# Attention with a gated feed-forward gate on one Trainium2 core: four-head groups outermost, transposes by DMA, 64-row scores and queries, and an opening by row tiles

## The chip, the cores and the metric

The kernel runs on one core of one Trainium2 chip. The time is the device time of a run in microseconds. In the profile PE is TensorE (matmuls), PEld its weight loads, DVE VectorE, ACT ScalarE, POOL GpSimd, SP the engine that only issues DMA. Runs of one kernel agree within 0.4%.

A profile shows one run; its span is the time from the first to the last instruction. The measured time of a run is a little longer than its span (957.23 against 955.5 us in the profiled run of the changed kernel).

## The reference, cut to what matters

```python
xn = layernorm(x)                                  # x: 2048 x 640, no affine part
q  = xn @ wq                                       # 32 heads of 192
k, v = k_cache[:, :, -512:], v_cache[:, :, -512:]  # the last 512 of 2048 positions
s  = softmax(q k^T / sqrt(192)) v  per head, then @ wo        # 6144 x 640
h  = sigmoid(xn @ w_gate) * (xn @ w_up)            # 640 x 1536 each
g  = silu(h @ w_down)
return x + s * g                                   # bf16 in and out
```

## The kernel before

It works in four blocks of 512 rows. A first part computes the layer norm, turns it (features onto the partitions) on TensorE, and does the whole gated feed-forward part. Then, block by block and inside a block head pair by head pair, `stage1` loads the pair's keys, values and query weights, makes the queries and turns the keys on TensorE; `stage_qk` makes scores and exps; `stage_pv` the weighted values. After the 16 pairs of a block `phase_a2` turns the outputs on TensorE and projects them. A head has 192 features: 128 of them are contracted in one full matmul, the remaining 64 in a matmul on 64 rows, and the two heads of a pair put their 64 rows into different halves of the array.

```python
    def stage1(st, hp, pair_idx):
        ...                                       # DMA: keys and values of two heads, 384 columns of wq
        for j in range(3):
            for c in range(NCD):                  # NCD = 5
                nc.tensor.matmul(q_ps[:], lhsT=wqp[:, c, j * P:(j + 1) * P],
                                 rhs=xnT_sb[:, c * 512:(c + 1) * 512], ...)
        ...
        for c in range(KC):                       # KC = 4: 12 key transposes a pair, in every block
            cb = c * 2 * DH
            for i in range(2):
                nc.tensor.transpose(kA_ps[:, i, c * P:(c + 1) * P], kt[:, cb + colA[i]:cb + colA[i] + P], ident[:])
            nc.tensor.transpose(kB_ps[:, c * P:(c + 1) * P], kt[:, cb + KPAD + P:cb + KPAD + 2 * P], ident[:])

    def stage_qk(st, ctxd):
        for c0 in range(0, KC, 2):
            for c in (c0, c0 + 1):
                for i in range(2):                # 4 matmuls of 128 rows
                    nc.tensor.matmul(S_ps[(c, i)][:], lhsT=kA[:, c * P:(c + 1) * P], rhs=qA_[:], start=True, stop=False)
            for c in (c0, c0 + 1):
                for i in range(2):                # 4 matmuls of 64 rows, heads in different halves
                    nc.tensor.matmul(S_ps[(c, i)][:], lhsT=kB[:, c * P:(c + 1) * P], rhs=qB_, start=False, stop=True)
            ...                                   # 4 exps of 512 columns

    def phase_a2(st):
        for q in range(TQ):
            for fq in range(NG):                  # 12 groups of 4
                for j in range(4):
                    nc.tensor.transpose(pT[:, j, :], o_st[q][:, cc * P:(cc + 1) * P], ident[:])
                ...                               # copy pT to oT, by VectorE and ScalarE in turn
                for j in range(4):
                    for (d0, dsz), oA_ps in zip(d_chunks, oA):    # 512 and 128 columns
                        nc.tensor.matmul(oA_ps[:], lhsT=oT[:, j, :], rhs=wo_sb[:, cc, d0:d0 + dsz], ...)
```

The softmax here doesn't subtract the row's maximum and nothing guards it: scores larger than these inputs give would overflow.

## Time and profile before

The median of three runs is 1075.28 us (1073.35 to 1076.93).

| | value | view |
|---|---|---|
| span | 1071.9 us | page |
| TensorE busy, ScalarE, VectorE | 97%, 48%, 41% | page, part 1 |
| chain of waits on TensorE | 82% | page, part 4 |
| until the first gate matmul | 11.76 us | timeline |
| one head pair | 9.64 us | timeline, distance of equal places |

The groups of instructions of the page, in the columns line, engine, operation, output and inputs, shape and count, then busy time and mean ns of one, then the idle time in front of them:

```profile
PE 1034.7 (97%) x7927; PEld 608.0 (57%) x8048; DVE 439.9 (41%) x1163; ACT 515.0 (48%) x981; POOL 113.9 (11%) x163
...
L236 PE MATMUL q_ps<-xnT_a,wqp 128*128 128x512 bf16 x901 | 214.9, 379 | 5.4 <-DMA wqp<-in_A_wq_dram 2.2
...
L343 PE MATMUL pTo<-ident,o_st 128*128 128x128 bf16 x768 | 54.0, 219 | 0.0
...
L254 PE MATMUL kA_ps<-ident,k_sb 128*128 128x128 bf16 x512 | 49.7, 219 | 0.0
L258 PE MATMUL kB_ps<-ident,k_sb 128*128 128x128 bf16 x256 | 46.2, 219 | 0.0
```

The lengths of matmuls overlap in the profile (their ends are modelled): a matmul of 379 ns is followed by the next after some 216 ns. What a matmul costs in a stream is the distance from start to start. The timeline of one score stage (start and length in us, then the instructions) shows it:

```profile
416.18 0.38 PE L286 MATMUL S_ps<-qT_3939,kTA 128*128 128x512 bf16 x1
...
416.39 0.38 PE L286 MATMUL S_ps<-qT_3955,kTA 128*128 128x512 bf16 x1
...
416.82 0.38 PE L286 MATMUL S_ps<-qT_3955,kTA 128*128 128x512 bf16 x1
...
417.13 0.60 PE L293 MATMUL S_ps<-qT_3947,kTB 64*128 64x512 bf16 x4
...
417.67 0.39 PE L286 MATMUL S_ps<-qT_3939,kTA 128*128 128x512 bf16 x1
```

Full 512-column matmuls start 0.21 us apart (0.2158 in the unbroken runs of query matmuls). The fourth full one starts at 416.82, but the first 64-row one only at 417.13, 0.31 us later. The four 64-row matmuls, two at a time, should take two such distances, 0.43 us; the next full one starts after 0.54. Each change between 128-row and 64-row matmuls so costs about 0.1 us in which nothing streams. The Trainium skill has this in "TensorEngine Tiling (Array Packing)", Key Properties: changing the tiling mode drains TensorE. It gives no figure; this trace does.

### The profile page before, as it was taken

The page shows a single profiled execution, that of the slowest core. Times are in us where ns is not written, and L with a number is a line of the kernel's source. Part 1 is how long each engine was busy: PE and PEld are TensorE (multiplying, and loading weights), DVE is VectorE, ACT ScalarE, POOL GpSimd, SP SyncE. Part 2 cuts the span into 40 slices and gives each one's busy share as a digit, 9 for nine tenths or more (in the row PEclk, how much of TensorE's full clock was granted, in tenths as well). Part 3 has the DMA queues.
Part 4 walks back from the last instruction along what each step waited for, and adds up shares of the span by engine and source line. Part 5 has one row for each costly group of instructions (what it writes and reads, how often), then busy time and mean ns, then how long its engine had stood idle before and what let it go on. Part 6 is the DMA issues. An engine that isn't in the chain of part 4 may idle for free.

```text
span 1071.9 us, 19547 instructions
## 1 busy us (share of the span) xinstructions
PE 1034.7 (97%) x7927; PEld 608.0 (57%) x8048; DVE 439.9 (41%) x1163; ACT 515.0 (48%) x981; POOL 113.9 (11%) x163
## 2 busy tenths in 40 slices
PE   6899999999999999999999999999999999999997
PEld 3445445556556665656556555656566555656664
DVE  4654333444454123544452224544432244544322
ACT  2654223666656114666653235666641165666321
POOL 4211002400010001000010010000000010000000
PEclk9999999999999999999999999999999999999999
DMA  9621002975555013555552024555521054451010
GB/s 303 196 93 50 13 37 77 343 205 130 135 127 163 20 38 78 133 144 131 137 144 65 20 71 127 129 144 132 136 70 38 20 147 127 129 144 50 1 38 13
DMA packets 153578, 115.18 MB, mean 107 GB/s; under 512 B 138000, under 2 KB 140560, under 8 KB 153488
## 3 DMA queue, kind: packets, MB, share of 16 engines
q1 hardware_dynamic: 138048, 53.63, 20.3%
q0 software_dynamic: 15440, 60.30, 18.8%
q8 instruction: 63, 1.03, 0.4%
q14 instruction: 27, 0.22, 0.1%
HBM read 106.04 MB, written 7.86 MB: 106 GB/s over the span
## 4 chain that ended last, share of the span: by engine, by line
PE 82%; issue 10%; DMA 3%; ACT 2%; POOL 2%; DVE 1%; POOLq 0%; DVEq 0%
PE q_ps L236 18%; PE o_ps L315 17%; PE S_ps L286 11%; PE S_ps L293 6%; PE kA_ps L254 3%; ACT oT L348 2%; PE pTo L343 2%; DMA xnT_d<-xnT_sb 1%; PE kB_ps L258 1%; PE g_ps L160 1%; PE u_ps L167 1%; PE oA_ps_4443 L352 1%; PE oA_ps_10299 L352 1%; PE oA_ps_13091 L352 1%; PE oA_ps_7371 L352 1%
## 5 line engine op out<-in xcount | busy, mean ns | idle before, releaser
L236 PE MATMUL q_ps<-xnT_a,wqp 128*128 128x512 bf16 x901 | 214.9, 379 | 5.4 <-DMA wqp<-in_A_wq_dram 2.2
L352 PEld LDWEIGHTS <-oT 128*128 128x128 bf16 x1536 | 115.3, 98 | 102.4 <-DVE oT L346 11.8
L328 DVE TENSOR_SCALAR o_st<-o_ps,rden 128x192 bf16<-128x192 f32 x384 | 148.3, 415 | 9.0
L348 ACT ACTIVATE oT<-pTo 128x512 bf16<-128x512 bf16 x96 | 53.8, 595 | 203.2 <-PE pTo L343 203.2
L236 PEld LDWEIGHTS <-wqp 128*128 128x128 bf16 x960 | 92.4, 97 | 100.8 <-DMA wqp<-in_A_wq_dram 2.7
L321 DVE RECIPROCAL rden<-o_ps 128x2 f32<-128x2 f32 x256 | 41.6, 162 | 192.9 <-PE o_ps L315 192.9
L346 DVE COPY oT<-pTo 128x512 bf16<-128x512 bf16 x96 | 40.7, 424 | 178.5 <-PE pTo L343 177.9
L228 POOL DMA_DIRECT2D wqp<-in_A_wq_dram x64 | 55.9, 874 | 472.5 <-PE q_ps L236 428.2
L326 ACT ACTIVATE o_st<-o_ps,rden 128x192 bf16<-128x192 f32 x128 | 54.0, 422 | 66.1 <-DVE o_st L328 61.2
L286 PEld LDWEIGHTS <-kTA 128*128 128x128 bf16 x512 | 42.1, 97 | 57.4 <-issue 26.7
L265 ACT ACTIVATE kTB<-kB_ps 128x512 bf16<-128x512 bf16 x64 | 38.2, 597 | 70.1 <-PE kB_ps L258 70.1
L160 PE MATMUL g_ps<-xnT_sb,wg_sb 128*128 128x512 bf16 x236 | 62.3, 384 | 1.8 <-DVE xnT_sb L154 1.3
L167 PE MATMUL u_ps<-xnT_sb,wu_sb 128*128 128x512 bf16 x233 | 60.8, 382 | 0.2
L173 ACT ACTIVATE sig_sb<-g_ps 128x512 bf16<-128x512 f32 x48 | 28.1, 597 | 60.9 <-PE g_ps L160 60.4
L174 DVE TENSOR_TENSOR hT_sb<-u_ps,sig_sb 128x512 bf16<-128x512 f32 x48 | 32.9, 690 | 53.8 <-PE u_ps L167 44.4
L343 PE MATMUL pTo<-ident,o_st 128*128 128x128 bf16 x768 | 54.0, 219 | 0.0
L254 PEld LDWEIGHTS <-k_sb 128*128 128x128 bf16 x512 | 42.0, 98 | 15.1
L343 PEld LDWEIGHTS <-o_st 128*128 128x128 bf16 x768 | 45.8, 98 | 7.6
L254 PE MATMUL kA_ps<-ident,k_sb 128*128 128x128 bf16 x512 | 49.7, 219 | 0.0
L258 PE MATMUL kB_ps<-ident,k_sb 128*128 128x128 bf16 x256 | 46.2, 219 | 0.0
L293 PEld LDWEIGHTS <-kTB 64*128 64x128 bf16 x512 | 14.6, 94 | 54.2 <-issue 54.2
L180 PEld LDWEIGHTS <-hT_sb 128*128 128x128 bf16 x384 | 29.8, 98 | 26.7 <-DVE hT_sb L174 3.5
(1006 smaller groups left out, 1839.0 us busy)
## 6 DMA issues: line engine op xcount, KB each, us to landing
wqp<-in_A_wq_dram POOLq DMA_DIRECT2D x64, 480.0 KB, 4.6
k_sb<-in_A_k_cache_dram SPq DMA_DIRECT2D x128, 192.0 KB, 4.8
wo_sb<-in_A_wo_dram POOLq DMA_DIRECT2D x16, 480.0 KB, 9.7
v_sb_96<-in_A_v_cache_dram SPq DMA_DIRECT2D x22, 192.0 KB, 2.9
v_sb_98<-in_A_v_cache_dram SPq DMA_DIRECT2D x22, 192.0 KB, 2.9
v_sb_100<-in_A_v_cache_dram SPq DMA_DIRECT2D x21, 192.0 KB, 2.9
v_sb_102<-in_A_v_cache_dram SPq DMA_DIRECT2D x21, 192.0 KB, 2.9
v_sb_104<-in_A_v_cache_dram SPq DMA_DIRECT2D x21, 192.0 KB, 2.9
```

The lines of the kernel that those rows point to most:

```text
L160: nc.tensor.matmul(g_ps[:], lhsT=wg_sb[:, c, f * P:(f + 1) * P], rhs=xnT_sb[:, c * 512:(c + 1) * 512], start=(c == 0), stop=(c == NCD - 1),)
L167: nc.tensor.matmul(u_ps[:], lhsT=wu_sb[:, c, f * P:(f + 1) * P], rhs=xnT_sb[:, c * 512:(c + 1) * 512], start=(c == 0), stop=(c == NCD - 1),)
L236: nc.tensor.matmul(q_ps[:], lhsT=wqp[:, c, j * P:(j + 1) * P], rhs=xnT_sb[:, c * 512:(c + 1) * 512], start=(c == 0), stop=(c == NCD - 1),)
L254: nc.tensor.transpose(kA_ps[:, i, c * P:(c + 1) * P], kt[:, cb + colA[i]:cb + colA[i] + P], ident[:],)
L258: nc.tensor.transpose(kB_ps[:, c * P:(c + 1) * P], kt[:, cb + KPAD + P:cb + KPAD + 2 * P], ident[:],)
L286: nc.tensor.matmul(S_ps[(c, i)][:], lhsT=kA[:, c * P:(c + 1) * P], rhs=qA_[:], start=True, stop=False,)
L293: nc.tensor.matmul(S_ps[(c, i)][:], lhsT=kB[:, c * P:(c + 1) * P], rhs=qB_, start=False, stop=True,)
L315: nc.tensor.matmul(o_ps[:, ii, 0:DH + 1], lhsT=E[i][:, c, q * P:(q + 1) * P], rhs=vt[:, c, 0:DH + 1], start=(c == 0), stop=(c == KC - 1),)
L328: nc.vector.tensor_scalar_mul(dst, o_ps[:, ii, 0:DH], rden[:, ii:ii + 1])
L343: nc.tensor.transpose(pT[:, j, :], o_st[q][:, cc * P:(cc + 1) * P], ident[:])
L348: nc.scalar.activation(oT[:], pT[:], AF.Copy)
L352: nc.tensor.matmul(oA_ps[:], lhsT=oT[:, j, :], rhs=wo_sb[:, cc, d0:d0 + dsz], start=(cc == 0), stop=(cc == NC_O - 1),)
```

## The change

The intent: take every transpose but the first block's off TensorE; load and turn each head's keys once instead of once per block, by putting groups of four heads outermost and the row blocks inside; contract all 192 features of a score in three steps of 64, two heads side by side, and split the query contraction likewise, so that TensorE changes its tiling twice per unit (four heads, 512 rows) instead of eight times for the same work; write the issue order by hand, with the projection of the unit before between the values of this one; begin with 128-row tiles, so that the first matmuls need one tile of x and one slice of weights. The diff, cut to its core:

```diff
+    ctx.enter_context(tc.manual_schedule())
+    bank = [psum.tile([P, 2, 512], F32, name=f"bank{i}") for i in range(4)]
+    def load_group(g):
+        d["wq"] = load2.tile([P, NCD, GW], BF16, name="wq_sb")
+        nc.gpsimd.dma_start(d["wq"][:], wq_r[:, :, g * GW:(g + 1) * GW])
+        ...                                  # one DMA for the keys of four heads, four for the values (GpSimd's queue)
+        for h in range(4):
+            nc.gpsimd.tensor_copy(kp[:, h // 2, :, :, (h % 2) * H2:(h % 2) * H2 + H2], ...)   # feature order 3 x 64
+    def turn_keys(g):
+        for pr in range(2):
+            for c in range(KC):
+                nc.sync.dma_start_transpose(d["kT"][:, pr, :, c * P:(c + 1) * P], d["kp"][:, pr, c, :, :]...)
 ...
-            nc.gpsimd.dma_start(wg_sb[:, :, f0:f1], wg_r[:, :, f0:f1])
-            nc.gpsimd.dma_start(wu_sb[:, :, f0:f1], wu_r[:, :, f0:f1])
+        for q in range(NF // 2):
+            load_slice(nc.scalar, wu_sb, wu_r, q)          # all six slices of w_up from ScalarE
+            if q:
+                load_slice(nc.sync, wg_sb, wg_r, q)
 ...
+        dummy(22)                                          # matmuls on zeros
+        ...
+        for t in range(TQ):                                # block 0: 128-row tiles, 4 of 12 feature groups
+            for f in range(FT): ...
+        for f in range(FT, NF):                            # block 0: the other 8, 512 rows
+            gated(0, f, 0, TB, k, norm_piece(1, f - FT))   # with half a tile's layer norm of block 1
+        load_group(0)
+        for b in range(1, NB): ...
 ...
+    def scores(u, pr, c, k):
+        for j in range(DJ):                                # DJ = 3
+            for i in range(2):
+                r = slice(i * H2, (i + 1) * H2)
+                nc.tensor.matmul(bank[k][:, i, :], lhsT=kT[r, pr, j, c * P:(c + 1) * P],
+                                 rhs=q[r, pr * DJ + j, :], start=(j == 0), stop=(j == DJ - 1))
+        nc.scalar.activation(E[u, pr][:, c, :, :], bank[k][:], AF.Exp, scale=scale_qk)   # 1024 columns
+    def queries(u, m, k, second):
+        for c in range(NCD):
+            for i in range(2):
+                half = i ^ second
+                n = 2 * m + half
+                col = (n // DJ) * 2 * DH + n % DJ
+                r = slice(i * H2, (i + 1) * H2)
+                nc.tensor.matmul(bank[k][:, half, :], lhsT=wq[r, c, col:col + DJ * (P - 1) + 1:DJ],
+                                 rhs=xnT[r, b, c, :], start=(c == 0 and not second), ...)
+    def turn_out(u):
+        for q in range(TQ):
+            nc.sync.dma_start_transpose(oT[u][:, :, q * P:(q + 1) * P], o_st[u][:, q, :])
 ...
+    for u in range(NU):                                    # 32 units
+        for i, what in enumerate(((0, 0), (1, 0), (0, 1), (1, 1), (2, 0), None, (2, 1), None)):
+            scores(u, *sc[i], i % 2)
+            if what is not None:
+                queries(u + 1, what[0], 2 + what[0] % 2, what[1])
+        ...
+            for q in range(4):
+                values(u, q, order[2 * q])
+                if u > 0:
+                    project(u - 1, q, order[2 * q + 1], nc.sync)
+            turn_out(u)
+    ...                                                    # last unit: project(u - 1, 1..3) after the values
```

## The prediction

> **What bounds it now.** TensorE. The page gives PE 97% busy of 1071.9 us, DVE 41%, ACT 48%; the cores view a clock of 0.999; the chain of waits is 82% PE. The timeline gives the pace: 512-column matmuls start 0.2155 us apart, 512+128 pairs of the output projection 0.272, 193-column value matmuls 0.085, transposes 0.056. Times the counts: queries 960 x 0.2155 = 207 us; scores 166 (512 full ones, and 512 on 64 rows that run two at once); values 173; output projection 209; gate and up 103; down 52; transposes 1596 x 0.056 = 89. Sum 999 us. The other 73 us are gaps: the opening until the first gate matmul (11.8 us in the timeline), a few waits (2.7 us at 44 us, a query-weight load that blocks from 182.9 to 190.5 us), about 0.1 us at each change between 128-row and 64-row matmuls (in the timeline 0.31 instead of 0.216 us going in, 0.54 instead of 0.43 for the four 64-row ones going out), and the end. The Trainium skill (TensorEngine Tiling (Array Packing), Key Properties) says a change of tiling mode drains TensorE; this trace agrees: four changes per head pair cost 0.41 us, over 64 pairs 26 us.
>
> **What changes.**
> - Removed from TensorE: 768 key transposes, 768 output transposes and 60 of 80 layer-norm transposes go to DMA: 1576 x 0.056 = 88 us.
> - Mode changes fall from 256 to about 64, because all scores and queries of a unit use 64 rows: 26 to about 6.5 us. 1536 + 1860 half matmuls, two at once, equal the full ones they replace.
> - Keys, values and query weights are loaded once, not four times; off the path but for that one stall.
> - Exps become 1024 wide, estimated at 0.6 + 512 x 0.83 ns = 1.03 us; eight per unit, 8.3 us against 11.7 us of score and query matmuls. DVE has about 11 us of work in a 23.5 us unit. Neither should bind before the last unit.
> - Added: waits for DMA transposes. They have half a unit (about 12 us) of slack, but block 1's last one is issued about 1 us before it is needed: estimate 2 to 3 us lost.
>
> **Sum.** 999 - 88 = 911 us of stream; opening about 9 plus 4 for weights that arrive late; block 1's wait 2.5; mode changes 6.5; small waits in 32 units 5; end 8 (exp-bound last scores, the last transpose, last output DMA). 946 us span; the measured time lies 3 us over the span. I predict 948 us, range 925 to 985. Nearly all removed time is critical, as PE is the chain.
>
> Chances: faster by over 2% 0.97, within 2% 0.02, slower 0.01.
>
> **What would show it.** PE's instruction count without the 1536 transposes; a unit of about 24 us repeated in the timeline; 64-row matmuls two per 0.216 us through a whole score-and-query phase; no PE idle blamed on ACT or DVE above a few us in the waits; DMA transposes landing in under 8 us; DMA traffic well below 115 MB.
>
> **What would make it wrong.** The query weights are now read with a column step of 3 and two 64-row loads per 0.216 us; no load in this trace is strided, and if they can't hide behind the matmuls, queries (a fifth of the time) slow down: +20 to +60 us. Long runs of 64-row pairs may not hold the pace that four show here. DMA transposes, all in one queue, four per unit, may take longer than the 12 us of slack. The opening may wait longer for weights.

## The result, and the profile after

The changed kernel takes 955.23 us (median of four runs, 954.33 to 957.23), the one before 1074.85 us in the same rounds. The ratio is 0.8885, with a 95% interval from 0.8869 to 0.8901. Ratios here are the mean time of one kernel's runs over that of the other's in the same rounds, so not quite the ratio of the medians quoted beside them. 948 us were predicted, and the range of 925 to 985 us holds the result.

The page after, in the same columns as before:

```profile
PE 924.1 (97%) x7965; PEld 551.0 (58%) x8045; DVE 470.6 (49%) x754; ACT 304.2 (32%) x339; POOL 131.6 (14%) x161
...
L360 PE MATMUL bank<-xnT,wq_sb 64*128 64x512 bf16 x1860 | 231.4, 376 | 0.0
...
L342 PE MATMUL bank<-qT,kT 64*128 64x512 bf16 x1536 | 202.4, 376 | 2.0 <-DVE o_st L383 1.3
L377 PE MATMUL bank<-vbuf,E 128*128 128x193 bf16 x2048 | 191.1, 247 | 0.0
```

The transpose groups are gone from TensorE. A matmul on 64 rows is recorded with the same 376 ns as a full one with 379; what tells is how close they lie, in the timeline of one score and query phase:

```profile
504.00 1.24 PE L360 MATMUL bank<-xnT,wq_sb 64*128 64x512 bf16 x10
505.08 1.46 PE L342 MATMUL bank<-qT,kT 64*128 64x512 bf16 x12
506.38 1.24 PE L360 MATMUL bank<-xnT,wq_sb 64*128 64x512 bf16 x10
507.46 0.81 PE L342 MATMUL bank<-qT,kT 64*128 64x512 bf16 x6
508.20 1.51 PE L377 MATMUL bank<-vbuf,E 128*128 128x193 bf16 x16
...
518.43 1.79 PE L400 MATMUL bank<-wo_sb,oT 128*128 128x512 bf16 x12
520.16 0.82 PE L342 MATMUL bank<-qT,kT 64*128 64x512 bf16 x6
```

Ten 64-row query matmuls, with their ten strided weight loads, take 1.08 us from start to start (505.08 minus 504.00): five times 0.216, so two at once for the whole phase. Twelve score matmuls take 1.30 us, six times 0.216. Only at the two ends is there a gap: the last six score matmuls should end at 507.46 + 0.65 = 508.11, the values start at 508.20; the projection that starts at 518.43 lasts 1.63, the scores start at 520.16. A unit repeats every 23.72 us (400.00 minus 376.28 in the chain of waits, for equal places); the matmuls of a unit alone are 54 x 0.2158 + 4 x 1.335 + 4 x 1.63 = 23.5 us (24 pairs of score matmuls and 30 of query matmuls, four heads' values, four projections). There is nothing left to win in a unit but the 0.2 us of the two changes of tiling.

What the prediction had not seen stands at the beginning. The waits, one line for each pair of instruction and what released it (total us, times, longest):

```profile
ACT xnT L207 <- DMA wu_sb<-in_B_w_up_dram: 8.9, 1, 8.9
PEld L221 <- DMA xnT<-xn: 11.6, 1, 11.6
PE bank L221 <- DMA xnT<-xn: 11.1, 1, 11.1
PE bank L221 <- DVE xnT L208: 5.7, 3, 4.9
```

TensorE waits once for a transpose of the layer norm, 11.1 us (its own line has 11.1, that of its weight load 11.6). And ScalarE waits 8.9 us, before the copy of the first turned tile, for a load of w_up which that copy does not read; 4.9 of TensorE's 5.7 us for VectorE's copy (last line) are the same wait one step on. The stretches of the opening (busy us of each engine, then the granted clock, the DMA share and its GB/s):

```profile
0.00:11.96 11.96, 5.89 (x30) 4.23 (x31) 3.18 (x10) 1.87 (x3) 1.43 (x10) 0.93 0.93 248
11.96:25.67 13.71, 12.87 (x176) 12.35 (x176) 8.50 (x31) 5.32 (x19) 1.65 (x3) 0.82 1.13 327
42.90:53.96 11.06, 0.00 (x0) 0.00 (x1) 0.69 (x1) 0.60 (x1) 3.72 (x5) 0.72 0.96 222
53.96:60.75 6.79, 6.74 (x23) 2.72 (x25) 0.69 (x1) 0.89 (x2) 3.13 (x4) 0.70 0.14 40
```

In the second and fourth stretch the granted clock is 0.82 and 0.70. In the trace's clock records it is half from 10.20 to 17.03 us and from 47.75 to 57.99 us, each time begun while TensorE idles. The Trainium skill, "TensorE: Matmul & The Clock Gate", Part 1, says just that: the clock falls to half after an idle window of about 3.4 us and comes back after as long a busy one. This trace agrees: 128-column matmuls start 0.107 us apart at 13 us and 0.056 at 18 us. So each long wait is paid for once more after it has ended, here with about 2.5 us (5.1 us of work at half clock from 11.96 on) and 2.0 us (4.0 us from 53.96 on).

### The profile page after: what moved, and what is told of

The parts are those of the page before. It is cut to its first block, busy times and chain, and to the rows that moved or that the text cites. A ratio compares the mean times of both kernels' runs of the same rounds, so it can differ in the third digit from the quotient of the medians. Undisturbed runs are those within 1.5% of the kernel's fastest.

```text
span 955.5 us, 18111 instructions
## 1 busy us (share of the span) xinstructions
PE 924.1 (97%) x7965; PEld 551.0 (58%) x8045; DVE 470.6 (49%) x754; ACT 304.2 (32%) x339; POOL 131.6 (14%) x161
## 2 busy tenths in 40 slices
DMA packets 159423, 76.69 MB, mean 80 GB/s; under 512 B 139120, under 2 KB 152688, under 8 KB 159344
## 3 DMA queue, kind: packets, MB, share of 16 engines
q8 instruction: 63, 1.03, 0.5%
## 4 chain that ended last, share of the span: by engine, by line
PE 94%; DMA 3%; DVE 1%; issue 1%; ACT 0%; SPq 0%; ACTq 0%
PE bank L360 21%; PE bank L400 21%; PE bank L377 18%; PE bank L342 17%; PE bank L221 11%; PE bank L233 5%; DMA xnT<-xn 1%; DMA oT<-o_st 1%; DMA wu_sb<-in_B_w_up_dram 1%; PE bank L307 1%; DMA x_sb<-in_A_x_dram 0%; DVE o_sb L405 0%; DVE hT L227 0%; ACT L346 0%; DVE o_sb L421 0%
## 5 line engine op out<-in xcount | busy, mean ns | idle before, releaser
L346 ACT ACTIVATE E<-bank 128x1024 bf16<-128x1024 f32 x256 | 257.9, 1023 | 479.6 <-PE bank L342 467.9
L360 PE MATMUL bank<-xnT,wq_sb 64*128 64x512 bf16 x1860 | 231.4, 376 | 0.0
L400 PE MATMUL bank<-wo_sb,oT 128*128 128x512 bf16 (+1 forms) x1461 | 223.8, 296 | 5.3 <-DMA oT<-o_st 1.9
L342 PE MATMUL bank<-qT,kT 64*128 64x512 bf16 x1536 | 202.4, 376 | 2.0 <-DVE o_st L383 1.3
L377 PE MATMUL bank<-vbuf,E 128*128 128x193 bf16 x2048 | 191.1, 247 | 0.0
L377 PEld LDWEIGHTS <-E 128*128 128x128 bf16 x2048 | 167.8, 98 | 24.3 <-issue 13.6
L367 DVE CAST qT<-bank 128x1024 bf16<-128x1024 f32 x93 | 113.9, 1224 | 133.5 <-PE bank L360 133.5
L360 PEld LDWEIGHTS <-wq_sb 64*128 64x128 bf16 x1860 | 97.2, 100 | 104.6
L342 PEld LDWEIGHTS <-kT 64*128 64x128 bf16 x1536 | 73.4, 94 | 91.8 <-issue 11.1
L383 DVE TENSOR_TENSOR o_st<-bank,rden 128x768 bf16<-128x768 f32 x128 | 122.5, 957 | 4.8 <-DVE rden L382 0.4
L411 DVE TENSOR_TENSOR acc<-bank,acc 128x640 f32<-128x640 f32 x96 | 79.1, 824 | 43.1 <-PE bank L400 42.9
L221 PE MATMUL bank<-xnT,wg_sb 128*128 128x512 bf16 (+1 forms) x296 | 63.7, 347 | 17.0 <-DMA xnT<-xn 11.1
L221 PEld LDWEIGHTS <-wg_sb 128*128 128x128 bf16 x300 | 27.9, 103 | 43.5 <-DMA xnT<-xn 11.6
```

The costliest lines, as they stand in the source:

```text
L221: nc.tensor.matmul(bank[k][:, half, 0:r1 - r0], lhsT=w[:, c, f * P:(f + 1) * P], rhs=xnT[:, b, c, r0:r1], start=(c == 0), stop=(c == NCD - 1))
L342: nc.tensor.matmul(bank[k][:, i, :], lhsT=kT[r, pr, j, c * P:(c + 1) * P], rhs=q[r, pr * DJ + j, :], start=(j == 0), stop=(j == DJ - 1))
L346: nc.scalar.activation(E[u, pr][:, c, :, :], bank[k][:], AF.Exp, scale=scale_qk)
L360: nc.tensor.matmul(bank[k][:, half, :], lhsT=wq[r, c, col:col + DJ * (P - 1) + 1:DJ], rhs=xnT[r, b, c, :], start=(c == 0 and not second), ...
L367: nc.vector.tensor_copy(qT[u][:, 2 * m:2 * m + 2, :], bank[k][:])
L377: nc.tensor.matmul(o4[:, q, 0:DH + 1], lhsT=e[:, c, h % 2, q * P:(q + 1) * P], rhs=v[:, h, c, 0:DH + 1], start=(c == 0), stop=(c == KC - 1))
```

## The experiments

Ten kernels were run, all correct. Chips differ between the three batches; the kernel before ran beside each batch (medians 1075.15, 1074.30 and 1075.43 us), and the changed kernel's 955.23 us stands for all comparisons with it.

### The gap before block 1

The timeline of the changed kernel before the gap (start, length, engine or issuing queue):

```profile
38.15 5.52 SPq L212 DMA_TRANSPOSE xnT<-xn  x2
...
41.29 0.55 POOL L191 TENSOR_TENSOR rstd<-rstd,mhalf 128x1 f32<-128x1 f32 x1 [3.71 <-DVE rstd L190]
...
41.84 1.05 POOL L96 DMA_DIRECT2D wq_sb<-in_A_wq_dram  x1
...
42.88 0.78 POOL L99 DMA_DIRECT2D k_st<-in_A_k_cache_dram  x1
...
43.66 2.96 POOL L105 DMA_DIRECT2D vbuf<-in_A_v_cache_dram  x4
```

```profile
DMA to landing us min/median/max: 2.6/2.6/11.4
```

The first line merges the last two transposes of block 1, the second of which is issued at about 42.5 us, just before it is needed at 42.9. GpSimd has finished its last small operation for block 1 at 41.84 and at once begins to issue the first head group's bulk load. The last line is from the view of the layer norm's tile: its DMA transposes land 2.6 us after issue as a rule, 11.4 us at most. The Trainium skill, "DMA: Bandwidth & Descriptors", Queues, rings and completion order, says that each DMA engine takes turns between the queues it has work for, a packet at a time. The packets in this trace agree for the longest part: the transposed tile is 672 packets of about 244 bytes (18 ns each); from 48 to 52 us 162 of them and 162 packets of the bulk load (about 190 ns each) were started, one for one. It is not so throughout: from 47 to 48 us it was 320 against 68. The two transposes before it, alone on the engines, started as many packets within 1 us. The keys' transposes of the same trace show the delay again: 29 of 64 overlap a GpSimd load of weights, keys or values and land after 6.5 us in the median, 8.7 at most; the other 35 after 2.4, 4.3 at most.

First experiment: a one-column copy on GpSimd that reads the transposed tile holds the bulk load until the tile has landed.

```diff
+        hold = bwork.tile([P, 1], BF16, name="hold", bufs=1)
+        nc.gpsimd.tensor_copy(hold[:], xnT[:, 1, 0, TB - 1:TB])
         load_group(0)
```

> The 11.06 us gap of TensorE before block 1 (42.9 to 54.0 us) ends on the DMA transpose of the block's last tile, which lands 11.4 us after its issue where the other layer-norm transposes take 2.6. Theory A: its roughly 670 packets of 256 bytes share the 16 DMA engines packet by packet with the first group's bulk load, which GpSimd issues from 41.8 us on; the load is held here until that transpose has landed. A expects the transpose to land about 2.6 us after its issue, the gap to shrink to 2 to 3 us, no half-clock stretch after it, and a time 10 to 12 us below the changed kernel (about 944 us). Rival B: the transpose queue itself is behind (the x loads and the 2 MB weight load ahead of it in the same queue, or the layer norm that feeds it). B expects the gap and the time unchanged within 1 us.

Measured: 946.92 us (945.29 to 947.31), 8.3 us less. The wait is 2.8 us instead of 11.1, the transposes land in 4.1 us at most:

```profile
PE bank L221 <- DMA xnT<-xn: 2.8, 1, 2.8
```

```profile
41.24:44.04 2.80, 0.00 (x0) 0.00 (x0) 0.69 (x1) 0.60 (x1) 0.00 (x0) 1.00 0.31 61
44.04:50.06 6.02, 6.01 (x20) 2.41 (x21) 0.69 (x1) 0.60 (x1) 4.92 (x7) 0.72 0.67 206
```

Theory A holds and B falls. The saving is smaller than expected, because after 2.8 us of idling the clock was still halved for 3.4 us, as the 0.72 in the second window shows.

Second experiment: nothing is held, but the bulk load goes into the queue of the transposes, behind the last one.

```diff
-    def load_group(g):
+    def load_group(g, eng=None):
+        eng = eng or nc.gpsimd              # its six DMAs are issued by eng
...
-        load_group(0)
+        load_group(0, nc.sync)
```

> The first group's bulk load goes through the same queue as the transposes, issued right behind the last transpose of block 1, with nothing held. Theory A in its narrow form (two queues take turns packet by packet, one queue keeps its order): the transpose lands in 2.6 to 4 us and the time falls by 9 to 12 us, as with the hold. Rival A2 (any bulk load in flight slows a transpose, whatever its queue): it lands in 8 to 11 us and the time stays within 2 us of the changed kernel. Rival B: unchanged.

Measured: 945.50 us (944.73 to 947.88), 9.7 us less. The transposes land in 3.2 us at most, although the bulk load is issued right behind the last one (from 42.71 us on). In one queue the order held: the transpose's last packet started at 43.70 us, the first of the bulk load at 43.95. So a bulk load behind the transpose in its own queue does not delay it, and A2's forecast (8 to 11 us) failed. A2's idea was not tested, since none of the load was moving while the transpose did; and the run changed two things, the queue and the order, as the load is now issued after the transpose and not before it (41.84 against 42.47 us). Shown is that a load ahead of it in another queue delays it. In this run the clock did not fall after the 2.8 us of waiting that were left.

### The opening

ScalarE issues six loads of w_up before anything else. From the timeline of the changed kernel:

```profile
1.18 1.04 ACTq L152 DMA_DIRECT2D wu_sb<-in_B_w_up_dram  x2
...
3.81 7.28 ACTq L152 DMA_DIRECT2D wu_sb<-in_B_w_up_dram  x4
...
5.86 0.74 PE L205 MATMUL bank<-ident,xn 128*128 128x128 bf16 x5
...
11.14 0.38 ACT L207 ACTIVATE xnT<-bank 128x256 bf16<-128x256 bf16 x1 [8.90 <-DMA wu_sb<-in_B_w_up_dram]
...
11.96 0.69 PE L221 MATMUL bank<-xnT,wg_sb 128*128 128x128 bf16 x5 [4.88 <-DVE xnT L208]
```

The tile is turned at 6.6 us, but its copy waits until 11.14 for ScalarE to have issued the last four loads, which took 7.28 us. The view has merged these four; asked for 3 to 9 us and for 9 to 11.5 us, it shows them apart:

```profile
3.81 0.37 ACTq L152 DMA_DIRECT2D wu_sb<-in_B_w_up_dram  x1
...
9.40 1.68 ACTq L152 DMA_DIRECT2D wu_sb<-in_B_w_up_dram  x3
```

So the issues themselves are short, 0.37 to 0.69 us each, and from 4.19 to 9.40 us ScalarE waited. In the trace's instruction records each of the last four waits for a semaphore that an earlier load of the opening uses too; that of the load at 9.40 is the one of a tile of x, which landed at 9.38. ScalarE stood behind the landing of earlier loads, by way of its own issues. In this experiment ScalarE issues two of the six and GpSimd the rest.

```diff
-            load_slice(nc.scalar, wu_sb, wu_r, q)
+            if q < 2:
+                load_slice(nc.scalar, wu_sb, wu_r, q)
...
         stats_end(0)
+        load_slice(nc.gpsimd, wu_sb, wu_r, 2)      # and 3
...
         stats_end(1)
+        load_slice(nc.gpsimd, wu_sb, wu_r, 4)      # and 5
```

> The first gate matmul starts at 11.96 us; ScalarE's copy of the first turned tile starts only at 11.14 us, behind ScalarE's own six weight-load issues, the last four of which take it 7.28 us. Four of the six move to GpSimd's queue. Theory C (the opening waits for ScalarE's issue slots, not for the weights): the copy runs at about 6.5 us, the first gate matmul starts at 8.7 to 9.5 us, when the first gate slice has landed, the clock does not fall to half between 10.4 and 17.3 us, and the time falls by 4 to 6 us. Rival D (the weights' arrival bounds the opening, DMA is 93% busy there): the copy is early but the first gates still wait for weights until about 11 us and the time falls by less than 1.5 us.

Measured: 951.87 us (950.31 to 952.33), only 3.4 us less, but the trace shows why:

```profile
6.59 0.39 ACT L208 ACTIVATE xnT<-bank 128x256 bf16<-128x256 bf16 x1 [4.35 <-PE bank L206]
...
7.69 0.44 PE L222 MATMUL bank<-xnT,wu_sb 128*128 128x128 bf16 x5
...
9.55 0.45 PE L222 MATMUL bank<-xnT,wg_sb 128*128 128x128 bf16 x5 [0.86 <-DMA wg_sb<-in_B_w_gate_dram]
```

```profile
PE bank L222 <- DMA xnT<-xn: 10.4, 1, 10.4
```

The copy runs at 6.59, the first gate matmul starts at 7.42 (8.7 to 9.5 were expected), the gated matmuls run at full clock (0.28 us for five, 8.25 minus 7.97), and the clock does not fall in the opening; of the waits for weights 0.9 us is left. At the gap before block 1 this kernel was 5.5 us ahead (37.4 instead of 42.9 us). The gap itself remained, 10.4 us, with 10.24 us of half clock from 40.50 on. Theory C holds, D falls. But the time fell by 3.4 us, not by 5.5 nor by the 4 to 6 expected, and what became of the other 2 us is open: in the profiled runs the spans differ by 7.0 us (948.5 against 955.5), in the three others of each by about 3 (950.3 against 953.4, the middle ones), and of those there is no trace. Their mean clock, 0.993 against 0.995 in the profiled run, hints at one more stretch at half clock (0.2% of 950 us is 1.9 us, an estimate).

Both changes together:

> The opening with four weight loads on GpSimd's queue, and the first group's load in the transposes' queue, together. If the two savings are independent: the sum of both, 3.4 + 9.7 = 13 us below the changed kernel, 942 us, and no less than 940. If what the opening won was mostly eaten by the gap before block 1 (there it was 10.4 us with 10 us of half clock after it), more: 938 to 941 us.

Measured: 940.82 us (940.69 to 942.19), 14.4 us below the changed kernel. The savings add up: 3.4 + 9.7 = 13.1, and the difference of 1.3 us is within what single runs vary. The run does not tell the two forecasts apart: 940.8 lies in both of their ranges.

And with block 1's layer norm two matmul groups earlier:

```diff
-            gated(0, f, 0, TB, k, norm_piece(1, f - FT))
+            todo = [norm_piece(1, i) for i in PIECES.get(f, ())]   # {4: (0,), 5: (1, 2), 6: (3,), 7: (4, 5), 8: (6,), 9: (7,)}
+            gated(0, f, 0, TB, k, lambda todo=todo: [do() for do in todo])
```

> As the run with both, and block 1's layer norm pieces are issued up to two matmul groups earlier, so that the last transpose has about 4.3 us more before it is needed. In both mended runs 2.8 us of waiting were left there, in one with a half-clock stretch after it. Expected: no TensorE wait for that transpose, 2.5 to 4.5 us below the run with both. Rival: VectorE cannot feed the norm pieces and the gated products at this pace, TensorE waits for it instead, no gain.

Measured: 938.39 us (937.26 to 939.58), 2.4 us below the run before it, just under the 2.5 to 4.5 expected. TensorE no longer waits for that transpose at all, and in the profiled run the clock is at full rate from its first record at 7.03 us to 935.46, 0.35 us before the end:

```profile
7.60:20.00 12.40, 10.50 (x175) 9.76 (x174) 8.29 (x30) 5.31 (x18) 3.39 (x5) 1.00 1.12 305
20.00:60.00 40.00, 39.74 (x219) 19.60 (x222) 19.31 (x43) 10.25 (x17) 5.87 (x9) 1.00 0.55 157
```

### Changes between 64 and 128 rows

Only the queries go back to 128-row matmuls. Their slots, banks and columns stay.

```diff
-        for c in range(NCD):
-            for i in range(2):
-                half = i ^ second
-                ...                                    # 10 matmuls on 64 rows, into both halves
+        n = 2 * m + second
+        col = (n // DJ) * 2 * DH + n % DJ
+        for c in range(NCD):                           # 5 matmuls on 128 rows, into one half
+            nc.tensor.matmul(bank[k][:, second, :], lhsT=wq[:, c, col:col + DJ * (P - 1) + 1:DJ],
+                             rhs=xnT[:, b, c, :], start=(c == 0), stop=(c == NCD - 1))
```

(The small read of the partial sum, which orders the two halves, reads one half.)

> One part undone: the queries run as full 128-row matmuls again, in the same slots between the 64-row scores, with the same columns streamed. Each of the six query slots of a unit then has a change of row tiling before and after it: 12 more per unit, 31 units. Theory E (each change costs about 0.1 us that nothing hides, as read from the kernel before): +37 us, range 30 to 45. Rival F (the 64-row queries gain nothing; the change of tiling is hidden or was an effect of the waits for banks in the kernel before): within 5 us of the changed kernel.

Measured: 996.10 us (995.57 to 998.00), 40.9 us more.

```profile
513.50 0.82 PE L342 MATMUL bank<-qT,kT 64*128 64x512 bf16 x6
514.25 1.26 PE L357 MATMUL bank<-xnT,wq_sb 128*128 128x512 bf16 x5
515.44 0.82 PE L342 MATMUL bank<-qT,kT 64*128 64x512 bf16 x6
```

Six score matmuls and what follows now take 0.75 us instead of 0.65 (514.25 minus 513.50), five query matmuls 1.19 instead of 1.08: 0.10 and 0.11 us for each change. With 31 x 12 = 372 changes, 40.9 us are 0.110 us each. Theory E holds, F falls. Splitting a full matmul into two 64-row halves costs nothing by itself, and pays as soon as its neighbours are 64-row matmuls.

### What the transposes by DMA are worth

Keys of groups 1 to 7 turned by TensorE, once per group:

```diff
+    def turn_keys_pe(g):
+        for pr in range(2):
+            v = wide(2 + pr).bitcast(BF16)[:, 0:DJ * W]...
+            for c in range(KC):
+                for j in range(DJ):
+                    nc.tensor.transpose(v[:, j, c * P:(c + 1) * P], d["kp"][:, pr, c, j, :], ident[:])
+            ...                                        # copied by ScalarE (pr 0) and VectorE (pr 1)
-        if b == 2 and g + 1 < NG:
-            turn_keys(g + 1)
...
             turn_out(u)
+            if b == 2 and g + 1 < NG:
+                turn_keys_pe(g + 1)
```

> One part undone: the keys of groups 1 to 7 are turned by TensorE again (24 transposes per group, between two units, into PSUM that is free there, copied by ScalarE and VectorE) instead of by DMA. Theory G (the 43 us of key transposes that the change removed are mostly due to turning each head's keys once instead of four times; turning them on TensorE once would cost 24 x 0.056 = 1.35 us a group plus up to 0.4 us of waiting for the copies): +9 to +13 us over the changed kernel, thus only about a quarter of the 43 us belongs to the DMA transposes. Rival H (the gain is due to the DMA transposes): +30 us or more.

Measured: 967.97 us (966.41 to 969.55), 12.7 us more, 1.8 us for each of seven groups. Theory G holds. Of the 43 us that the key transposes cost before (768 x 0.056), the larger part, 32 us of stream (576 transposes), is the doing of the loop order, which turns each head's keys once instead of four times. The DMA transposes account for the rest: of the 12.7 us, 9.4 are the stream of seven groups (7 x 1.35), and about 3 are waits around them.

Outputs of the first 31 units turned by TensorE:

```diff
+    def turn_out_pe(u):
+        for pr in range(2):
+            v = wide(2 + pr).bitcast(BF16)[:, 0:GC * 2 * P]...
+            for q in range(2):
+                for cc in range(GC):
+                    nc.tensor.transpose(v[:, cc, q * P:(q + 1) * P], o_st[u][:, 2 * pr + q, cc * P:(cc + 1) * P], ident[:])
+            ...                                        # copied by ScalarE (pr 0) and VectorE (pr 1)
-            turn_out(u)
+            turn_out_pe(u)
```

> One part undone: the attention outputs of the first 31 units are turned by TensorE (24 transposes of 128x128 per unit after its last projection, into two free double banks, copied once by ScalarE and once by VectorE, 1536 columns each) instead of by DMA. The prediction's term for these 768 transposes was 768 x 0.056 = 43 us. If TensorE's stream is the only limit: +42 us (31 x 1.34), up to +56 if the next unit's queries also wait some 0.4 us for the copy that frees their bank. Rival: DMA transposes are not free for the rest of the kernel (they hold up loads or the projections), and giving them up returns something: +30 us or less.

Measured: 1004.62 us (1003.72 to 1005.78), 49.4 us more.

```profile
541.02 1.50 PE L397 MATMUL bank<-ident,o_st 128*128 128x128 bf16 x24
542.46 0.82 PE L342 MATMUL bank<-qT,kT 64*128 64x512 bf16 x6
543.39 1.26 PE L360 MATMUL bank<-xnT,wq_sb 64*128 64x512 bf16 x10
```

The 24 transposes take 1.44 us (542.46 minus 541.02), and the first queries start 0.93 us after the scores instead of 0.65, as they wait for the copy that frees their bank. Together that is 1.7 us, and 49.4 / 31 = 1.6. The DMA transposes of the outputs give nothing back elsewhere: they are the largest single part of the gain.

### The end

The three projections of unit 30 back in front of the last values:

```diff
+    for q, k in ((1, 1), (2, 2), (3, 3)):
+        project(u - 1, q, k, nc.scalar)
-    for h, k in enumerate((1, 2, 3, 0)):
+    for h, k in enumerate((0, 1, 2, 3)):
         values(u, h, k)
     turn_out(u)
-    for q, k in ((1, 1), (2, 2), (3, 3)):
-        project(u - 1, q, k, nc.scalar)
```

> One part undone: the three projections of unit 30 that the change runs after the last values, while the last outputs are turned by DMA, run before the last values again. Theory J (they fill 4.9 us in which TensorE would wait for those transposes; ahead of the values they fill some 1 to 1.5 us in which it waits for the last exps): +3 to +4 us over the changed kernel, and a new TensorE wait of 4 to 6 us for the last transposes. Rival: the end is bound by the last transposes and outputs anyway, within 1 us.

Measured: 960.73 us (960.27 to 961.54), 5.5 us more. The new wait is there:

```profile
PE bank L400 <- DMA oT<-o_st: 4.8, 2, 4.2
```

It is 4.8 us in two waits against 1.9 us in the changed kernel, 2.9 us more. And the long wait halved the clock: the records have it at half from 945.35 to 948.76 us, 1.7 us more for the same work. From the first scores of the last unit to the end it took 36.5 us instead of 32.0, which these two account for. The expectation was too low, since the projections filled nothing in front of the values (TensorE's only wait for an exp, 0.6 us, is in the first unit), and since it had not counted the clock.

Last, on top of the early norm pieces, the three final partial outputs in three double banks:

```diff
-                ps = bank[(k + i // 2) % 4][:, i % 2, 0:d1 - d0]
+                ps = bank[(k + i) % 4][:, 0, 0:d1 - d0]
```

> On top of the run with the early norm pieces: the three last partial outputs go to three different double banks. Until now the second part waits 1.45 us until VectorE has read the first, though they lie in different halves of one double bank. Expected: that wait is gone from the waits; the time falls by 0.4 to 1.5 us only, because VectorE's own six operations on the parts follow one another anyway.

Measured: 937.18 us (936.56 to 937.92). The wait of 1.45 us is gone from the list. The median is 1.2 us lower than in the run without it, on another chip. The intervals of the two ratios (0.8714, from 0.8700 to 0.8728, and 0.8736, from 0.8723 to 0.8749) overlap, so the gain in time is not settled. Why two parts in different halves of one double bank had to wait for each other was not tried. This kernel is the fastest of all, 0.8714 of the one before; the changed one is at 0.8885.

## Why the prediction was right

The mechanism and the size were right: 948 us predicted, 955.2 measured. Point by point:

- *Stream of 999 us less 88 us of transposes.* Right. Where nothing waits, the changed kernel runs at the predicted pace: 17.23 us for the 80 matmuls from 25.67 to 42.90 us, 23.72 us for a unit with 23.5 us of stream. Undoing the output transposes cost 49.4 us (43 were predicted as stream; the rest is the wait for copies, which the kernel before had in its own way), undoing those of the keys 12.7 us. What the prediction left out is that three quarters of the key transposes go away by the loop order, whatever engine turns them.
- *Mode changes, 256 to 64 at 0.1 us: 26 to 6.5 us.* Right. The experiment gives 0.110 us for each, so 192 fewer are worth 21 us.
- *The strided weight loads and long runs of 64-row matmuls*, named as dangers, did no harm: ten query matmuls take 1.08 us.
- *Small waits of 5 us in the units.* Too high by half: from 192.37 to about 923.4 us, 731 us, against 31 x 23.72 less the 6.52 us of projections that the first unit does not have, 728.8 us. The difference of 2.2 us is all in the first unit (192.37 to 211.80 us, 19.4 instead of 17.2).
- *Opening about 9, plus 4 for weights that arrive late.* The sum was near (15.9 us against 13), the reason wrong, and so it was near by luck. The first gate matmul starts at 11.96 us, and the stretch after it takes 13.71 us where 160 gated matmuls and 15 transposes at 0.056 us need 9.8. It was not the weights of these matmuls: ScalarE's copy waited behind its own DMA issues, which waited for earlier loads to land, and the idle time halved the clock. With the issues moved, the first gate matmul starts at 7.42 us.
- *Block 1's wait, 2 to 3 us.* This is the term that was mis-sized. It was 11.1 us, and 2.0 us more at half clock: 13.1 us. The kernel before has no transpose by DMA, so the estimate had no measurement behind it, and it took the landing time for that of a transfer alone. It did not ask which transfers are issued at the same moment, though the order of issue stands in the code: GpSimd reaches the bulk load as soon as its last small operation for block 1 is done. With the load in the transpose's own queue, the wait is the 2.8 us that were predicted.
- *End, 8 us.* Near: from 923.4 us to the end 32 us, against 23.5 us of stream. But the last exps do not bind it: TensorE waits for none of them.
- *Exps of 1.03 us.* Right: the trace before has 597 ns for ScalarE's 512 columns and 277 for 128, hence 0.83 ns a column; the 1024 wide exps took 1.024 us.
- *The measured time lies 3 us over the span.* It was 1.8 us, which changes nothing.
- *What would show it.* Most held: the unit, the pace, no waits for ScalarE or VectorE in the units, 76.69 MB instead of 115.18. Two did not. The count of TensorE's instructions does not fall (8045 weight loads against 8048): 1596 transposes went, but 1442 halves of matmuls, 120 matmuls for the opening's row tiles, 25 on zeros and 6 in the split last projection came. And not every transpose landed in under 8 us: three took 8.2, 8.7 and 11.4.

The gain of 119.6 us is then, by these experiments: about 49 us for turning the outputs by DMA, 13 us for turning the keys by DMA, 32 us of stream for turning them once (worked out, not run), 21 us for fewer changes of tiling (worked out from the measured 0.110 us), 5.5 us for the projections in the tail; and the opening with its two waits gave some of it back. Smaller parts are 3 us of stream for the layer norm's tiles (60 x 0.056, worked out) and the 2.2 us that TensorE waited for query weights before 190.48 us. The row tiles of the opening and the issue order by hand were not undone by themselves; as it stood the opening gained nothing, the first gate matmul starts at 11.96 us against 11.76 before. The parts were measured one at a time on the changed kernel, and need not add up exactly.

## What to carry to other kernels

When a transfer that TensorE is about to need is small and made of many small packets, look at what else is issued to DMA at that moment: put the bulk behind it in the same queue, or hold it until the small one has landed. Keep DMA issues that may have to wait for earlier loads off the queue of an engine that has to do the first piece of compute. And keep matmuls of one row tiling together: each change cost 0.11 us here, and nothing ran on TensorE meanwhile.

## What the Trainium skill lacked or had wrong

- "TensorEngine Tiling (Array Packing)", Key Properties, says that a change of tiling mode drains TensorE but not how long: 0.110 us for each of 372 changes here.
- "DMA: Bandwidth & Descriptors", Queues, rings and completion order, has the taking of turns packet by packet, but not what it does to a transpose: 672 packets of 244 bytes landed in 2.6 us alone and in 11.4 us beside a bulk load in another queue.
- No page that I found says what it costs when loads share a few semaphores, so that one is not issued before an earlier one has landed: ScalarE's last four loads of the opening, 1.9 us of issuing, held it for 7.28 us, and SP's five held it for 8.24 us.
- "TensorE: Matmul & The Clock Gate", Back-to-back issue gap, gives 131 ns as the sustained spacing of 512-column matmuls with their weight loads. Here it is 215.8 ns in unbroken runs of query matmuls at full clock, which agrees with the page's isolated figure of 215.7.
- The same page, Part 1, has the clock fall after an idle window of about 3.4 us, and says that the window runs freely. In each run here the changes of the clock indeed lie whole multiples of 3.413 us apart, but a window need not be idle throughout: gaps of 2.8 us (the held load) and 2.3 us (both changes together), each inside one window, were followed by 3.4 us at half clock, while 2.8 us split over two windows, 1.9 and 1.0 (the load in the transposes' queue), were not.
